# Casting x to bf16 in the load instead of on the engines, in a kernel of small attention blocks and a gated feed-forward stage

## The chip, the cores and the metric

The kernel runs on one core of a Trainium2 chip. Five engines work side by side, each through its own queue in order: PE (TensorE, matmuls and transposes), DVE (VectorE), ACT (ScalarE), POOL (GpSimd) and SP (SyncE, here only a queue for transfers). Data move between the chip's memory and the on-chip buffers by 16 DMA engines, which SP, ACT and POOL feed. A transfer that SP issues copies bytes as they are or transposes bf16 blocks; one that POOL issues can change the type on the way. The metric is the device time of one execution, in microseconds (us).

## The reference

There are two parts: an attention of x and a small state in both directions, batch by batch and head by head, and a gated feed-forward stage over all rows that come out. x is (8, 8, 512, 64): batch, head, token, width; state is (8, 8, 32, 64).

```python
scores = scale * x @ state^T          # (B, H, 512, 32)
xread  = softmax(scores) @ state      # (B, H, 512, 64)
scores2 = scale * state @ x^T         # the same products, transposed
sread  = softmax(scores2) @ x         # (B, H, 32, 64)
attn   = concat([xread, sread], axis=2)            # 544 rows for each head
x      = attn.transpose(0, 2, 1, 3).reshape(8 * 544, 512)
out    = (sigmoid(x @ w_gate) * (x @ w_val)) @ w_out   # 512 -> 1536 -> 512
```

Inputs and output are float32; the kernel computes its matmuls in bf16.

## The kernel before

**Tiling.** A batch is one unit of 512 token rows. Tokens lie as p*4 + c, with p the partition and c from 0 to 3. Heads go in pairs: j counts the four pairs, e the head in a pair. For each batch the kernel makes:

- xf, x in float32 (loaded by `load_x`), and xb, its bf16 copy with the heads in a row (`cast_x`; one call handles some of the heads on one engine);
- xT, its transpose: for batches 0 and 1 by PE (`xT_mm`) and a copy out of PSUM (`xT_cp`), from batch 2 on by SP's transposing transfers (`at_xT_dma`);
- the scores S (`S_mm`), with xT as the stationary operand and the moving one sTz, which is the state transposed with zeros so that a pair of heads gives two separate blocks; then exp on ACT (`S_exp`);
- Eb, the exponentials in bf16 (`at_Eb`, POOL), sums over the state's rows and their reciprocals (`n_sum`, DVE), the normalised a (`n_mul`) and its transpose aT (`aT_mm` and `aT_cp`, or by SP's transfers);
- SW, the state times the gate and value weights (`sw_mm`, called by `sw_visit` or `sw_wide`; copied out of PSUM by `sw_cp`), so that x's read never has to be formed: the gate and value inputs of a batch are aT times SW (`gv_mm`), followed by tanh (`gv_th`, ACT) and a product (`gv_glu`, DVE), and by the last matmul (`out_mm`);
- for the state's rows, sr (`sr_mm`, with Eb and xb), divided by the sums (`sr_fin`) into XS, which goes through the feed-forward stage at the end as "batch 8". For batch 1 the sums over tokens are first made on POOL (`p_tok`).

The state is loaded for two batches at a time (q counts these). For q = 0 it comes in float32 by ACT's queue and is cast; the others come as bf16 by POOL's queue (`load_sb`). `sT_mm` transposes it on PE by a matmul with the identity, and `sT_cp` or `sT_pad` copies it from PSUM into sTc (plain) or sTz (padded). `pad` copies sTc into sTz on POOL.

**The order.** The schedule is manual: the order in which the code calls these functions is the order in each engine's queue, and the framework adds the semaphores. Lines 434 to 652 write the order out by hand for batches 0 and 1 and the way into batch 2; the loop at line 654 runs the steady state, in which each batch's gv and out matmuls are interleaved with the next batch's preparation. PSUM tiles come from four pools, named GV (2 buffers), SWP (4), AT (1) and OU (1) in the calls, and a matmul into a buffer waits until its last reader is done. `warm` issues matmuls with no use of their own on PE before data are there. `gate` is a tiny POOL copy that reads one element, so that what POOL issues behind it waits for that element.

**Where the change and the steps of the prediction lie.** In the opening SP issues x of batches 0 and 1 in four parts each (lines 435 and 436), POOL casts a part of x and the state and then issues the weight loads, and DVE and ACT cast the other parts of x (lines 404 to 445). Lines 445 to 485 hold the first scores, Eb, the loads, the products `n_mul(1, ...)` on POOL and `aT_mm(1)`. Lines 503 to 555 hold the `sw_visit` calls, `sr_mm(1)`, `sT_mm(3)` and `sT_mm(1)`, and x of batch 2. Lines 576 to 599 lead to the first `out_mm` and the scores of batch 2.

Of the kernel before, what the change touches and what calls it, by code (L numbers as in the profile page):

```python
# [8 lines left out]
FP = mybir.dt.float32  # L9
BF = mybir.dt.bfloat16  # L10
# [6 lines left out]
def kernel(  # L17
# [14 lines left out]
    nc = tc.nc  # L32
# [32 lines left out]
    xfs, xbs, xTs = {}, {}, {}  # L65
# [4 lines left out]
    def load_x(b, eng, parts=1):  # L70
        xf = xfs[b] = stg.tile((128, H, 4, D), FP, name="xf")
        v, n = x[b].rearrange("h (p c) d -> p h c d", c=4), H // parts
        for i in range(parts):
            eng.dma_start(xf[:, n * i:n * i + n], v[:, n * i:n * i + n])  # L74

    def load_w(w, lo, n):
        src = (moe_w_gate, moe_w_val)[w].rearrange("(k p) n -> p k n", p=128)
        nc.gpsimd.dma_start((wg, wv)[w][:, :, lo:lo + n], src[:, :, lo:lo + n])

    def gate(landed):  # L80

        nc.gpsimd.tensor_copy(pre[:, 1:2], landed)
# [5 lines left out]
    def cast_x(b, cp, lo, n):  # L88
        if b not in xbs:
            xbs[b] = xp.tile((128, 4, H, D), BF, name="xb")  # L90
        cp(xbs[b].rearrange("p c h d -> p h c d")[:, lo:lo + n], xfs[b][:, lo:lo + n])  # L91


    def xT_tile(b):
# [6 lines left out]
    def xT_mm(b, j, place):  # L101

        ps = held["xT", b, j] = place[0].tile((128, 4, 128), BF, name="xTp", tag=place[1])
        for c in range(4):
            nc.tensor.transpose(ps[:, c], xbs[b][:, c, 2 * j:2 * j + 2].rearrange("p h d -> p (h d)"), ident)  # L105

    def xT_cp(b, j, cp):
        cp(xT_tile(b)[:, j], held["xT", b, j])  # L108
# [1 line left out]
    def at_xT_dma(b):  # L110
        xT = xT_tile(b)
        for c in range(4):
            nc.sync.dma_start_transpose(xT[:, :, c], xbs[b][:, c].rearrange("p h d -> p (h d)"))

    def S_mm(b, i, place, jjs=(0, 1)):
        if jjs[0] == 0:
            held["S", b, i] = place[0].tile((128, 4, 2, 2, Ns), FP, name="Sp", tag=place[1])
        ps = held["S", b, i]
        for jj in jjs:
            for c in range(4):  # L120
                nc.tensor.matmul(ps[:, c, :, jj], xTs[b][:, 2 * i + jj, c], sTz[:, b, 2 * i + jj], start=True, stop=True)  # L121

    def S_exp(b, i):
        if b not in E1s:
# [4 lines left out]
    def at_Eb(b):  # L129
        Ebs[b] = ap_.tile((128, 4, 2, 4, Ns), BF, name="Eb")  # L130
        for c in range(4):
            nc.gpsimd.tensor_copy(Ebs[b][:, c], E1s[b][:, c])  # L132
# [36 lines left out]
    def n_mul(b, i, eng, lo=0, n=4):  # L169
        if b not in abs_:  # L170
            abs_[b] = ap_.tile((128, 4, 2, 128), BF, name="ab")
        ri, ce = held["ri", b, i], slice(2 * lo, 2 * lo + 2 * n)
        eng.tensor_tensor(abs_[b].rearrange("p c e (j n) -> p (c e) j n", n=Ns)[:, ce, 2 * i:2 * i + 2],  # L173
                          halfE(b, i)[:, ce], ri[:, ce].unsqueeze(3).to_broadcast((128, 2 * n, 2, Ns)), ALU.mult)

    def aT_mm(b, place):
        ps = held["aT", b] = place[0].tile((128, 4, 2, 128), BF, name="aTp", tag=place[1])
        for c in range(4):
            for e in range(2):
                nc.tensor.transpose(ps[:, c, e], abs_[b][:, c, e], ident)  # L180
# [48 lines left out]

    sw_left = {}  # L230

    def sw_mm(pss, b, w, lo, n, o):
        for j in range(4):
            for e in range(2):
                rows = slice(e * 64, (e + 1) * 64)
                nc.tensor.matmul(pss[e][j * Ns:(j + 1) * Ns, o:o + n], sTc[rows, b, j] if b > 1 else sTz[rows, b, j, e],  # L236
                                 (wg, wv)[w][rows, j, lo:lo + n], start=True, stop=True)

    def sw_visit(b, lo, n, *ws):
# [126 lines left out]
    def cast_s(q, cp):  # L366
        sbs[q] = stg.tile((128, 1, 4, D), BF, name="sb", bufs=4)
        cp(sbs[q], sfs[q])

    def sT_mm(q, place):  # L370
        ps = stp[q] = place[0].tile((128, 4, 64), FP, name="stp", tag=place[1])
        for l in range(4):
            for e in range(2):
                nc.tensor.matmul(ps[e * 64:(e + 1) * 64, l], sbs[q][:, 0, l], ident_e[:, e], start=True, stop=True)
# [4 lines left out]
    def sT_pad(q, e, cp):  # L379

        rows = slice(e * 64, (e + 1) * 64)
        cp(sTz[rows, 2 * q:2 * q + 2, :, e].rearrange("p b j (u l) -> p (b j) u l", u=8),
           stp[q][rows].rearrange("p l (g u) -> p g u l", u=8))

    def pad(b, n=1):
        for e in range(2):
# [351 lines left out]
```

## Time and profile before

| | us |
|---|---|
| median of three runs | 226.21 (225.6 to 226.31) |
| the profiled execution | 226.03 |
| its span | 224.2 |
| PE busy in it | 217.0 (97%) |
| DVE busy | 140.7 (63%) |
| ACT busy | 127.6 (57%) |
| POOL busy | 48.8 (22%) |

The granted TensorE clock is 1.00 over the whole execution. The profile is one execution; its lines give times in us from the span's start. A line such as "11.23 1.44 POOL L132 CAST Eb<-E ... x4" is four instructions of line 132 on POOL that read E and write Eb, from 11.23 for 1.44 us; brackets behind it give the idle time in front of it and what ended that. A busy PE is modelled, so what counts on PE is where its stream stops. Landing times of transfers are counted from their issue.

### The profile page before, as it was taken

How to read it: one execution, taken by the hardware profiler on the slowest of the kernel's cores; microseconds unless marked ns; L12 is line 12 of the kernel's file. 1: busy time of each engine (PE TensorE's matmuls, PEld its weight loads, DVE VectorE, ACT ScalarE, POOL GpSimd, SP SyncE). 2: the span in 40 equal slices, each digit the busy share in tenths (PEclk: the TensorE clock that was granted, in tenths of full speed). 3: DMA queues.
4: the chain of work that ended last, by engine and by line, in shares of the span. 5: the costliest groups of instructions: out<-in, count | busy, mean ns of one | idle time of the engine just before them, and what ended most of it. 6: DMA issues, size and time to landing. Idle time of an engine off the chain costs nothing.

```text
span 224.2 us, 4791 instructions
## 1 busy us (share of the span) xinstructions
PE 217.0 (97%) x1859; PEld 111.2 (50%) x1859; DVE 140.7 (63%) x248; ACT 127.6 (57%) x239; POOL 48.8 (22%) x85
## 2 busy tenths in 40 slices
PE   7789999999999999999999999999999999999994
PEld 6654444444444545454444454454445444466744
DVE  3599897779368756885488648864787434422311
ACT  2587885645676557656675667556755444423311
POOL 3799560362041004200240006000200000000001
PEclk9999999999999999999999999999999999999999
DMA  6999989753898352627362521253122111111114
GB/s 188 289 201 206 280 130 179 114 193 78 147 292 274 71 151 76 219 59 126 100 225 50 121 96 61 44 81 117 47 78 66 50 50 47 67 73 48 50 26 114
DMA packets 38566, 27.37 MB, mean 122 GB/s; under 512 B 21168, under 2 KB 33840, under 8 KB 38544
## 3 DMA queue, kind: packets, MB, share of 16 engines
q1 hardware_dynamic: 31392, 19.74, 32.5%
q0 software_dynamic: 6864, 7.14, 17.6%
q8 instruction: 14, 0.23, 0.4%
q10 hardware_dynamic: 288, 0.20, 0.3%
q14 instruction: 8, 0.07, 0.1%
HBM read 18.35 MB, written 8.91 MB: 122 GB/s over the span
## 4 chain that ended last, share of the span: by engine, by line
PE 91%; DVE 3%; DMA 2%; ACT 1%; SPq 1%; issue 0%
PE outp L319 38%; PE gvp L288 37%; PE swp L236 5%; PE gvp L291 5%; DMA xf<-in_x_dram 2%; PE srp L213 1%; PE Sp L121 1%; PE outp L339 1%; DVE rs L139 1%; PE srp L210 1%; SPq L74 1%; DVE ab L173 1%; DVE ri L141 0%; DVE r L218 0%; PE xTp L105 0%; PE warm L353 0%
## 5 line engine op out<-in xcount | busy, mean ns | idle before, releaser
L303 DVE SCALAR_TENSOR_TENSOR glu<-th,gvp 128x512 bf16<-128x512 f32 (+1 forms) x108 | 69.9, 655 | 64.0 <-ACT th L298 48.7
L319 PE MATMUL outp<-wo,glu 128*128 128x512 bf16 x396 | 98.2, 379 | 0.0
L288 PE MATMUL gvp<-aT,SW 128*128 128x512 bf16 x384 | 96.3, 379 | 0.3 <-DVE aT L190 0.2
L298 ACT ACTIVATE th<-gvp 128x512 f32<-128x512 f32 (+1 forms) x108 | 61.8, 574 | 60.6 <-PE gvp L288 49.2
L288 PEld LDWEIGHTS <-SW 128*128 128x128 bf16 x384 | 36.3, 98 | 44.7 <-issue 3.1
L319 PEld LDWEIGHTS <-glu 128*128 128x128 bf16 x396 | 37.4, 98 | 40.8 <-issue 0.4
L274 ACT CAST SW<-swp 128x512 bf16<-128x512 f32 x70 | 38.8, 586 | 4.7 <-PE swp L236 3.3
L132 POOL CAST Eb<-E 128x256 bf16<-128x256 f32 x32 | 11.5, 407 | 89.9 <-ACT E L126 89.9
L323 ACT ACTIVATE res<-outp 128x512 f32<-128x512 f32 x33 | 19.7, 597 | 17.6 <-PE outp L319 17.6
L274 DVE CAST SW<-swp 128x512 bf16<-128x512 f32 x26 | 17.1, 683 | 1.6 <-PE swp L236 1.4
L91 POOL CAST xb<-xf 128x1024 bf16<-128x1024 f32 (+1 forms) x13 | 13.8, 1093 | 12.1 <-DMA xf<-in_x_dram 10.7
L330 POOL DMA_DIRECT2D out_dram<-res x2 | 1.1, 542 | 60.0 <-ACT res L323 60.0
L147 DVE TENSOR_REDUCE E<-E 128x128 f32<-128x512 f32 x12 | 12.4, 1035 | 0.0
L139 DVE TENSOR_REDUCE rs<-E 128x16 f32<-128x512 f32 x16 | 10.8, 676 | 1.3 <-ACT E L126 1.3
L126 ACT ACTIVATE E<-Sp 128x512 f32<-128x512 f32 x16 | 9.6, 604 | 2.4 <-PE Sp L121 2.4
L173 DVE TENSOR_TENSOR ab<-E,ri 128x512 bf16<-128x512 f32 x12 | 9.6, 804 | 0.0
L236 PE MATMUL swp<-wg,sTc 64*32 64x512 bf16 (+1 forms) x192 | 8.4, 328 | 0.0
L236 PEld LDWEIGHTS <-sTc 64*32 64x32 bf16 x384 | 4.5, 91 | 7.4 <-issue 4.7
L218 DVE RECIPROCAL r<-srp 128x128 f32<-128x128 f32 x8 | 7.6, 950 | 0.0
L121 PEld LDWEIGHTS <-xT 128*128 128x128 bf16 x128 | 5.5, 98 | 4.0 <-DVE xT L108 1.0
L236 PE MATMUL swp<-wv,sTc 64*32 64x512 bf16 (+1 forms) x192 | 7.4, 322 | 0.0
L291 PE MATMUL gvp<-XS,wg 128*128 128x256 bf16 x48 | 7.2, 273 | 0.0
(64 smaller groups left out, 122.0 us busy)
## 6 DMA issues: line engine op xcount, KB each, us to landing
out_dram<-res SPq DMA_DIRECT2D x31, 256.0 KB, 2.6
xf<-in_x_dram SPq DMA_DIRECT2D x12, 256.0 KB, 4.5
xf<-in_x_dram SPq DMA_DIRECT2D x3, 1024.0 KB, 6.8
wo<-in_moe_w_out_dram POOLq DMA_DIRECT2D x3, 512.0 KB, 5.9
wg<-in_moe_w_gate_dram POOLq DMA_DIRECT2D x2, 512.0 KB, 9.2
wv<-in_moe_w_val_dram POOLq DMA_DIRECT2D x2, 512.0 KB, 10.8
xf<-in_x_dram POOLq DMA_DIRECT2D x2, 512.0 KB, 10.4
xf<-in_x_dram POOLq DMA_DIRECT2D x1, 1024.0 KB, 9.2
```

The source lines that it names most:

```text
L91: cp(xbs[b].rearrange("p c h d -> p h c d")[:, lo:lo + n], xfs[b][:, lo:lo + n])
L139: nc.vector.tensor_reduce(rs, halfE(b, i), AX.X, ALU.add)
L147: nc.vector.tensor_reduce(held["E4", b][:, e].rearrange("p j n -> p (j n)"), E1s[b][:, :, e].rearrange("p c j n -> p (j n) c"), AX.X, ALU.add)
L173: eng.tensor_tensor(abs_[b].rearrange("p c e (j n) -> p (c e) j n", n=Ns)[:, ce, 2 * i:2 * i + 2], halfE(b, i)[:, ce], ri[:, ce].unsqueeze ...
L236: nc.tensor.matmul(pss[e][j * Ns:(j + 1) * Ns, o:o + n], sTc[rows, b, j] if b > 1 else sTz[rows, b, j, e], (wg, wv)[w][rows, j, lo:lo + n] ...
L274: cp(*sw_left.pop((b, lo, w, e)))
L288: nc.tensor.matmul(ps, SWs[b][:, g, w, fs], aTs[b][:, :, g], start=(g == 0), stop=(g == 1))
L291: nc.tensor.matmul(ps, (wg, wv)[w][:, j, fs], XS[:, j], start=(j == 0), stop=(j == 3))
L298: nc.scalar.activation(th, held["gv", b, f][0], AF.Tanh, scale=0.5)
L303: nc.vector.scalar_tensor_tensor(glus[b][:, f], held["th", b, f], 1.0, held["gv", b, f][1], ALU.add, ALU.mult)
L319: nc.tensor.matmul(ops[b, c], glus[b][:, f, c * 128:(c + 1) * 128], wo[:, f], start=(f == 0), stop=(f == NF - 1))
L323: nc.scalar.activation(res, ops[b, c], AF.Copy, scale=0.5)
```

## The change

The file has a second form of x in bf16, xc, laid out by head: (128, head, c, width). It is filled by `load_xc`, a POOL transfer that casts on the way. The table CP says which pairs of heads of which batch are held in that form: pairs 2 and 3 of batch 0, and all of batches 1 to 3. For these, SP issues no load, and xb is copied from xc on POOL at a later place, since `sr_mm` still reads it. The transposes read xc directly; with its layout a block of 128 columns holds two token positions of one head, not one token position of two heads, so `S_mm` takes another moving operand, sTd, with the head's state in both halves of the partitions, in separate column blocks. `sT_mm` makes both forms where both are needed, and `sT_dup` copies the new one out of PSUM. For q = 1 only the new form is made, and at another place in the order; sr_mm(1), wo's first load, some casts and the first three weight loads also stand in other places. The gate in front of the fourth weight load is gone.

```diff
+    CP = {0: (2, 3), 1: (0, 1, 2, 3), 2: (0, 1, 2, 3), 3: (0, 1, 2, 3)}
+    sTd = wp.tile((128, len(CP), H, 2, Ns), BF, name="sTd")
...
+    def load_xc(b, lo, n):
+        if b not in xcs:
+            xcs[b] = xp.tile((128, H, 4, D), BF, name="xc", bufs=len(CP))
+        v = x[b].rearrange("h (p c) d -> p h c d", c=4)
+        nc.gpsimd.dma_start(xcs[b][:, lo:lo + n], v[:, lo:lo + n])
...
     def cast_x(b, cp, lo, n):
-        cp(xbs[b].rearrange("p c h d -> p h c d")[:, lo:lo + n], xfs[b][:, lo:lo + n])
+        cp(xbs[b].rearrange("p c h d -> p h c d")[:, lo:lo + n],
+           (xcs[b] if lo // 2 in CP.get(b, ()) else xfs[b])[:, lo:lo + n])
...
     def xT_mm(b, j, place):
         for c in range(4):
-            nc.tensor.transpose(ps[:, c], xbs[b][:, c, 2 * j:2 * j + 2].rearrange("p h d -> p (h d)"), ident)
+            if j in CP.get(b, ()):
+                blk = xcs[b][:, 2 * j + c // 2, c % 2 * 2:c % 2 * 2 + 2].rearrange("p c d -> p (c d)")
+            else:
+                blk = xbs[b][:, c, 2 * j:2 * j + 2].rearrange("p h d -> p (h d)")
+            nc.tensor.transpose(ps[:, c], blk, ident)
...
     def at_xT_dma(b):
+            if b in CP:
+                nc.sync.dma_start_transpose(xT[:, c], xcs[b][:, 2 * c:2 * c + 2].rearrange("p h c d -> p (h c d)"))
...
     def S_mm(b, i, place, jjs=(0, 1)):
+                j, e, k = 2 * i + jj, c // 2, c % 2
+                if j in CP.get(b, ()):
+                    nc.tensor.matmul(ps[:, 2 * k:2 * k + 2, e, jj], xTs[b][:, j, c],
+                                     sTd[:, list(CP).index(b), 2 * j + e], start=True, stop=True)
...
     def sT_mm(q, place):
+        n = 0 if q == 1 else 32 if q == 0 else 64
+        if q < 2:
+            h0 = 64 - 8 * len(CP.get(0, ())) * 2 if q == 0 else 0
+            sd = stp[q, "d"] = ps[:, 4 * n:4 * n + 4 * (128 - h0)].rearrange("p (l g) -> p l g", l=4)
...
+                if n:
+                    nc.tensor.matmul(sz[rows, l], sbs[q][:, 0, l], ident_e[:, e, :n // 8], start=True, stop=True)
+                if q < 2:
+                    nc.tensor.matmul(sd[rows, l], sbs[q][:, 0, l], ident[:, h0:], start=True, stop=True)
...
+    def sT_dup(q, e, cp):
+        rows = slice(e * 64, (e + 1) * 64)
+        sd = stp[q, "d"][rows].rearrange("p l (g u) -> p g u l", u=8)
+        g = sd.shape[1]
+        hi = 8 * (2 * q + 2 - min(CP))
+        cp(sTd.rearrange("p b h e n -> p (b h) e n")[rows, hi - g:hi, e].rearrange("p g (u l) -> p g u l", u=8), sd)
...
     load_s(0, nc.scalar)
-    load_x(0, nc.sync, 4)
-    load_x(1, nc.sync, 4)
+    load_x(0, nc.sync, 4, 2)
     make_identity(nc, ident)
+    load_xc(0, 4, 4)
+    load_xc(1, 0, 4)
+    load_xc(1, 4, 4)
+    load_w(1, 256, 256)
+    load_w(0, 256, 256)
+    load_w(0, 0, 256)
...
+    nc.vector.memset(sTd, 0.0)
...
-    cast_x(0, pool, 0, 2)
+    cast_s(0, act)
+    cast_x(0, act, 0, 2)
...
-    cast_s(0, pool)
-    load_w(1, 256, 256)
     sT_mm(0, OU)
     sT_pad(0, 1, vec)
-    cast_x(0, act, 6, 2)
+    sT_dup(0, 0, vec)
+    sT_dup(0, 1, vec)
...
-    cast_x(0, act, 4, 2)
-    load_w(0, 256, 256)
-    load_w(0, 0, 256)
-    cast_x(1, vec, 2, 2)
-    gate(xfs[0][:, 7, 0, 0:1])
-    cast_x(1, act, 0, 2)
-    cast_x(1, vec, 4, 2)
-    cast_x(1, pool, 6, 2)
     at_Eb(0)
+    cast_x(0, pool, 4, 4)
...
     n_mul(1, 0, nc.gpsimd)
+    cast_x(1, pool, 0, 4)
+    cast_x(1, pool, 4, 4)
...
-    load_x(2, nc.gpsimd, 2)
+    load_xc(2, 0, 8)
+    load_wo(0)
     p_tok(1)
...
     sw_visit(0, 1024, 512, 0)
-    sr_mm(1, OU)
...
-    sT_mm(1, GV)
-    load_wo(0)
-    sT_cp(1, vec)
...
-    cast_x(2, act, 0, 4)
+    cast_x(2, pool, 0, 4)
     cast_x(2, pool, 4, 4)
     sw_visit(0, 512, 512, 1)
     gv_mm(1, 11, SWP)
+    sr_mm(1, OU)
...
     gv_glu(0, 7)
+    sT_mm(1, AT)
     gv_glu(0, 10)
+    sT_dup(1, 0, vec)
+    sT_dup(1, 1, act)
...
-    pad(2, 6)
+    pad(4, 4)
...
-    load_x(3, nc.gpsimd)
+    load_xc(3, 0, 8)
```

In the diff, lines of one function or stretch that lie apart are shown together. `sw_mm` takes the state of batches 1 to 3 from sTd as well.

More of the change, by code (lines that the diff above doesn't have):

```diff
@@ L120, in S_mm @@
             for c in range(4):
-                nc.tensor.matmul(ps[:, c, :, jj], xTs[b][:, 2 * i + jj, c], sTz[:, b, 2 * i + jj], start=True, stop=True)
+                j, e, k = 2 * i + jj, c // 2, c % 2
+                if j in CP.get(b, ()):
+                    nc.tensor.matmul(ps[:, 2 * k:2 * k + 2, e, jj], xTs[b][:, j, c],
+                                     sTd[:, list(CP).index(b), 2 * j + e], start=True, stop=True)
+                else:
+                    nc.tensor.matmul(ps[:, c, :, jj], xTs[b][:, j, c], sTz[:, b, j], start=True, stop=True)
     def S_exp(b, i):
@@ L230, with s_of @@
     sw_left = {}
+    def s_of(b, j, e):
+        rows = slice(e * 64, (e + 1) * 64)
+        if len(CP.get(b, ())) == 4:
+            return sTd[rows, list(CP).index(b), 2 * j + e, e]
+        return sTc[rows, b, j] if b > 1 else sTz[rows, b, j, e]
     def sw_mm(pss, b, w, lo, n, o):
@@ L235, in sw_mm @@
                 rows = slice(e * 64, (e + 1) * 64)
-                nc.tensor.matmul(pss[e][j * Ns:(j + 1) * Ns, o:o + n], sTc[rows, b, j] if b > 1 else sTz[rows, b, j, e],
+                nc.tensor.matmul(pss[e][j * Ns:(j + 1) * Ns, o:o + n], s_of(b, j, e),
                                  (wg, wv)[w][rows, j, lo:lo + n], start=True, stop=True)
@@ L370, in sT_mm @@
     def sT_mm(q, place):
-        ps = stp[q] = place[0].tile((128, 4, 64), FP, name="stp", tag=place[1])
+        n = 0 if q == 1 else 32 if q == 0 else 64
+        ps = place[0].tile((128, 512), FP, name="stp", tag=place[1])
+        sz = stp[q] = ps[:, :4 * n].rearrange("p (l g) -> p l g", l=4) if n else None
+        if q < 2:
+            h0 = 64 - 8 * len(CP.get(0, ())) * 2 if q == 0 else 0
+            sd = stp[q, "d"] = ps[:, 4 * n:4 * n + 4 * (128 - h0)].rearrange("p (l g) -> p l g", l=4)
         for l in range(4):
             for e in range(2):
-                nc.tensor.matmul(ps[e * 64:(e + 1) * 64, l], sbs[q][:, 0, l], ident_e[:, e], start=True, stop=True)
+                rows = slice(e * 64, (e + 1) * 64)
+                if n:
+                    nc.tensor.matmul(sz[rows, l], sbs[q][:, 0, l], ident_e[:, e, :n // 8], start=True, stop=True)
+                if q < 2:
+                    nc.tensor.matmul(sd[rows, l], sbs[q][:, 0, l], ident[:, h0:], start=True, stop=True)
     def sT_cp(q, cp):
@@ L381, in sT_pad @@
         rows = slice(e * 64, (e + 1) * 64)
-        cp(sTz[rows, 2 * q:2 * q + 2, :, e].rearrange("p b j (u l) -> p (b j) u l", u=8),
+        cp(sTz[rows, 0, :, e].rearrange("p j (u l) -> p j u l", u=8),
            stp[q][rows].rearrange("p l (g u) -> p g u l", u=8))
+    def sT_dup(q, e, cp):
+        rows = slice(e * 64, (e + 1) * 64)
+        sd = stp[q, "d"][rows].rearrange("p l (g u) -> p g u l", u=8)
+        g = sd.shape[1]
+        hi = 8 * (2 * q + 2 - min(CP))
+        cp(sTd.rearrange("p b h e n -> p (b h) e n")[rows, hi - g:hi, e].rearrange("p g (u l) -> p g u l", u=8), sd)
     def pad(b, n=1):
```

9 lines of the change are left out of this document (5 added, 4 removed).

## The prediction

> **What bounds the kernel now.** I read the page first for the engine that has no room, then the chain for where that engine begins to run without a pause, then the timelines around the two places that the change touches.
>
> ```profile
> PE 217.0 (97%) x1859; PEld 111.2 (50%) x1859; DVE 140.7 (63%) x248; ACT 127.6 (57%) x239; POOL 48.8 (22%) x85
> PE   7789999999999999999999999999999999999994
> DMA  6999989753898352627362521253122111111114
> ```
> PE is the bound, and only the first three slices (some 17 us) leave it idle. The profiled execution took 226.03 us, its span 224.2, so 1.83 us lie around the span. The median of the runs shown is 226.21, 0.18 higher. From 18 us on, the table by stretches shows PE busy all the time except 0.1 us near 28.3, up to the tail. So the time is: when PE's unbroken run starts, plus the work in that run, plus any new pause. The chain of waits (start, length, engine and line) shows what comes before the run:
>
> ```profile
> 2.27 5.24 DMA xf<-in_x_dram
> 7.53 0.63 ACT xb L91
> 8.21 0.40 PE xTp L105 x4
> 9.64 0.42 PE Sp L121 x8
> 10.09 0.60 ACT E L126
> 17.90 0.61 PE aTp L180 x8
> ```
> Batch 0's last x block lands at 7.5, is cast on ACT, transposed, scored at 9.64; after much DVE work PE starts aT_mm(1) at 17.90 and never stops. What holds aT_mm(1) is seen in the timelines of POOL and PE, which add the operation and, in brackets, the idle time before it and what ended it:
>
> ```profile
> 11.23 1.44 POOL L132 CAST Eb<-E 128x256 bf16<-128x256 f32 x4 [0.23 <-ACT E L126]
> 12.60 0.54 POOL L364 DMA_DIRECT2D sb<-in_state_dram  x1
> 13.13 0.75 POOL L78 DMA_DIRECT2D wg<-in_moe_w_gate_dram  x1
> 13.86 1.50 POOL L78 DMA_DIRECT2D wv<-in_moe_w_val_dram  x2
> 15.35 2.09 POOL L173 TENSOR_TENSOR ab<-E,ri 128x512 bf16<-128x512 f32 x2
> ...
> 15.92 0.30 PE L236 MATMUL swp<-wv,sTz 64*32 64x256 bf16 x8 [0.20 <-DMA wv<-in_moe_w_val_dram]
> 16.40 1.02 PE L288 MATMUL gvp<-aT,SW 128*128 128x512 bf16 x4 [0.18 <-DVE aT L190]
> ```
> POOL runs from E's end (11.2) to 17.44 with no hole; aT_mm(1) needs its last product. A weight load (15.92) and a DVE copy (16.40) stand only a little ahead of that. The third place is later:
>
> ```profile
> 25.27 0.41 PE L236 MATMUL swp<-wv,sTz 64*32 64x512 bf16 x8
> 25.50 0.40 PE L236 MATMUL swp<-wg,sTz 64*32 64x512 bf16 x8
> 25.83 0.40 PE L210 MATMUL srp<-Es,ones 128*128 128x128 bf16 x4
> 26.06 0.63 PE L213 MATMUL srp<-Eb,xb 128*128 128x64 bf16 x16
> 26.53 1.03 PE L288 MATMUL gvp<-aT,SW 128*128 128x512 bf16 x4
> 28.04 0.44 PE L374 MATMUL stp<-ident,sb 128*64 128x64 bf16 x16
> ...
> 25.75 1.07 ACT L274 CAST SW<-swp 128x512 bf16<-128x512 f32 x2
> 27.96 1.07 ACT L274 CAST SW<-swp 128x512 bf16<-128x512 f32 x2 [0.20 <-PE swp L236]
> ...
> 26.87 0.18 PEld L288 LDWEIGHTS <-SW 128*128 128x128 bf16 x2 [0.25 <-ACT SW L274]
> ```
> The matmul of sw_visit(1, 512, 512, 1) at 25.27 lets ACT cast from 25.75 to 26.83, and gv_mm(1, 7)'s third matmul must wait for that cast: its weights load at 26.87, just in time. PE's 0.70 us of sr_mm(1) at 25.83 fills exactly this wait. Likewise the 0.13 us of sT_mm(1) at 28.2 (half of the sixteen) ends as ACT's cast at 27.96 frees the buffers of the next gv_mm, at 28.55.
>
> **The change, part by part.**
>
> *First x block.* SP issues two parts instead of eight. POOL is free at 1.30 (identity done) and issues heads 4 to 7. Lower bound of the landing: load_wo(1), on a nearly idle queue, took 5.9 us from issue for twice the bytes; the extra 256 KB at the 200 GB/s seen from 10 to 16 us are 1.3, so 4.6, hence 5.9. Upper: the first weight load of the same size, with x beside it, took 6.4, hence 7.7. Here only 640 KB of SP's and ACT's loads stand beside it, and the middle, 6.9, is taken. The ACT casts (0.62 each) leave that path: transposes and their end 0.8 after landing, 7.7.
>
> *DVE in front of the scores.* Before, two pads of 64x256 took 0.86. Now two pads of half that and two copies of 64x384 from PSUM: 128x256 took 0.41 and 128x512 0.69, so about 0.28 and 0.55 each, 1.66. From the end of DVE's cast (5.46) that is 7.1; two copies of xT (0.74) 7.85; the third (0.42) 8.27. So DVE, not the load, decides: scores at 8.3 against 9.64, 1.35 earlier (at a landing of 7.7, 0.7). The state's cast and one x cast on ACT, idle until 7.53, and the second memset (0.91) on DVE, idle from 2.2 to 4.9, cost nothing. Sixteen instead of eight state matmuls lie in the time when PE runs warm-ups.
>
> *POOL.* Ahead of E it now has eight loads of 0.75, done by 7.5, without the gate. After E (now 9.9) come Eb 1.37, the new cast_x(0) of 128x1024 (1.04 for f32 to bf16 in this trace; a bf16 copy of 64x768 took 0.84, so no cheaper), the state 0.53, three loads 2.22, two products 2.09: 17.15 instead of 17.44. So 1.04 of the 1.35 are spent here, 0.3 is left. Behind the products wait batch 1's two casts (2.03), the state loads, x of batch 2, and p_tok(1) with Eb(1), done about 27; their reader sr_mm(1) comes after 31, and sr_fin(1) frees its buffer from 38.7 on as before. wo's first part goes ahead of p_tok(1); its reader starts at 40.26.
>
> *Weights.* POOL's queue, whose first packets came 3.3 after the issue at 5.12 (at 8.5 by the transfers in short windows), now moves from about 4.6, with x in front: 1.83 MB up to the fourth weight load at 0.2 MB/us is 13.8, and that load's lag behind its bytes before was 1.5: 15.3 against 15.9. PE could then begin aT_mm(1) near 17.2, so POOL (17.15 plus the 0.45 seen from its end to the first matmul) still ends last: 17.6 against 17.90. **Start: -0.3**, bounds +0.35 (late landing) and -0.7 (weights).
>
> *sr_mm(1) moved* behind gv_mm(1, 11), where PE's 44 matmuls from 30.75 to 40.05 follow without a gap. There it costs its whole length, 0.70 (between 53.71 and 54.40 its like takes 0.69). Where it leaves, PE waits for ACT instead. Bounds 0 (if ACT came ahead) and 0.70; ACT's cast hangs on PE's own matmul at 25.27, so **+0.70**.
>
> *sT_mm(1) moved* and widened to 128 columns. Its old place gains nothing (ACT's end at 28.55 holds the next matmul). In the new one: 0.31 from a 512-column matmul into such a group (20.75 to 21.05), three steps of 0.056, 0.31 out (28.29 to 28.60), less the 0.22 of one step: 0.57; at least 0.22. Taken: **+0.57**. Its two copies (0.7 on DVE, 0.6 on ACT) stand where DVE idles 1.0 us near 35.3 and replace sT_cp(1) and ACT's cast of x, 1.04.
>
> *Rest.* Batch 2's and 3's transposes by DMA no longer wait for a cast; scores of batch 2 stand at 41.98 and had their xT at 39.5. POOL's pads, x of batch 3 in bf16 and the other weight rows keep their shapes and lie beside PE: 0.
>
> Sum: -0.30 + 0.70 + 0.57 = +0.97, so 226.03 + 0.97 = 227.0.
>
> **Two rules.** The Trainium skill, "DMA: Bandwidth & Descriptors", Anatomy of one DMA, gives a load issued from GpSimd about 2.0 us plus bytes over 436 GB/s; an estimate by it for load_wo(1), 1 MB read, is 4.4, and the trace has 5.9, so the rule is short by 1.5 here. By it the landing would be 4.5, rival B would fall away, and the sum would stay 227.0, since DVE decides. "SBUF — State Buffer", Who interferes with whom, says that a DVE copy in a two-port mode shuts GpSimd out; DVE's x cast beside POOL's took 0.54 against 0.42 here, which agrees. By it that cast, now beside POOL's descriptor writing, would shift the weights by up to 0.5 and give 227.2.
>
> **Rivals.**
> A, the forecast: 226.6 to 227.6.
> B, heads 4 to 7 land late. For it: the 6.4 us row. Against: less stands beside it. From 7.0 on each us counts; at 7.7 the scores gain 0.7, POOL's cast costs 1.04, the start loses 0.35: 226.03 + 0.35 + 1.27 = 227.65.
> C, not slower: ACT's cast at 25.75 comes ahead, so that sr_mm(1) covered nothing. It decides if that cast ends 0.5 us or more earlier against PE. Against it: ACT was idle 0.1 before it, waiting for PE. Time 226.03 - 0.3 + 0.57 = 226.3.
> D, POOL's cast isn't last, since its spans are rough: start -0.7, 226.03 - 0.7 + 1.27 = 226.6.
> E, the whole 1.35 of the scores reaches aT_mm(1) (POOL not last, and the weights' lag 0.8 instead of 1.5, as the first x part's was) and C holds, with sT_mm(1) at 0.22: 226.03 - 1.35 + 0.22 = 224.9; faster.
>
> **Numbers.** A 0.58, B 0.18, C 0.08, D 0.06, E 0.10. A measurement of this kernel tells about 0.3% (0.7 us) from no change: 225.5 to 226.9. Of A two thirds lie above 226.9. Slower: 0.39 + 0.18 = 0.57; same: 0.19 + 0.08 + 0.06 = 0.33; faster 0.10. The range runs from between C and E to beyond B: 225.9 to 228.2; A's own is 226.6 to 227.6.
>
> **What would show it.** Scores of batch 0 near 8.3, with DVE's xT copies just ahead; POOL busy from 9.9 to 17.2 and aT_mm(1) released by it near 17.6; an idle PE of about 0.7 before the third matmul of gv_mm(1, 7), released by ACT; srp matmuls after 31 with no idle time ahead. The prediction is wrong if PE's run starts before 17 or after 18.3, if that 0.7 isn't there, or if PE pauses anew between 31 and 45, where xT of batch 2, the state copies or wo come late.

## The result, and the profile after

The changed kernel takes 228.65 us (median of 4 runs, 228.41 to 229.9), the kernel before 225.91 (4 runs, 225.23 to 226.31): ratio 1.0136, 95% interval 1.0089 to 1.0183. The change costs 2.7 us. Two of its four executions, 228.85 and 229.9, ran at a mean granted clock of 0.99, the other two, 228.41 and 228.45, at 1.00. The sign was forecast; the size was not, since 228.65 lies above the range. The profiled execution took 228.41 us with a span of 226.6: 2.38 us more than the profiled execution of before.

The page of the changed kernel, busy time and two rows by slices:

```profile
PE 217.8 (96%) x1867; PEld 111.2 (49%) x1867; DVE 143.1 (63%) x249; ACT 126.9 (56%) x238; POOL 52.4 (23%) x87
PE   7779899899999999999999999999999999999994
DMA  6999989593799253527471421244122111111113
```

PE's work rose by only 0.8 us; the rest is idle time: slices 3, 5 and 8 are each a tenth less busy than before, all others as they were. The chain of waits (start, length, engine and line) names the places:

```profile
10.42 1.44 POOL Eb L154 x4
11.86 0.99 POOL xb L100
...
14.79 12.78 DMA wv<-in_moe_w_val_dram
...
32.13 0.47 PE srp L235 x16
...
38.44 0.60 DVE sTd L428
39.04 0.02 issue
39.06 0.59 ACT sTd L428
...
44.45 1.02 PE outp L347 x4
```

PE's own timeline, with the idle time before each group in brackets, gives the pauses:

```profile
25.41 0.40 PE L264 MATMUL swp<-wg,sTz 64*32 64x512 bf16 x8
25.74 0.60 PE L316 MATMUL gvp<-aT,SW 128*128 128x512 bf16 x2
26.79 0.61 PE L316 MATMUL gvp<-aT,SW 128*128 128x512 bf16 x2 [0.45 <-ACT SW L302]
27.61 0.41 PE L264 MATMUL swp<-wv,sTz 64*32 64x512 bf16 x8 [0.21 <-DMA wv<-in_moe_w_val_dram]
...
31.97 0.63 PE L235 MATMUL srp<-Eb,xb 128*128 128x64 bf16 x16
32.44 5.34 PE L316 MATMUL gvp<-aT,SW 128*128 128x512 bf16 x24
37.71 0.41 PE L411 MATMUL stp<-ident,sb 128*64 128x128 bf16 x8
...
44.45 1.02 PE L347 MATMUL outp<-wo,glu 128*128 128x512 bf16 x4 [0.57 <-DVE glu L331]
```

Setting the start of each matmul against the same matmul of before gives the account of the two profiled executions:

| Place (time before) | shift so far | added here |
|---|---|---|
| gv_mm(0, 3) (16.41), aT_mm(1) (17.90) | -0.09 | -0.09 |
| sw_visit(0, 1024, 512, 1) (27.49), waits for the last wv load | +0.12 | +0.21 |
| after sr_mm(1) (31.75 after) | +0.81 | +0.69 |
| after sT_mm(1) (37.71 after) | +1.25 | +0.44 |
| out_mm(0, 7) (42.45), waits for DVE's glu | +2.00 | +0.75 |
| PE's last matmul (221.13) | +2.00 | 0 |
| end of the span | +2.4 | +0.4 |

Everything happens before 45 us or in the last 4. From out_mm(0, 7) on, the two kernels run in step.

### The profile page after: what moved, and what is told of

It reads as the page before. It is cut to its first block, busy times and chain, and to the rows that moved or that the text cites. A ratio compares the mean times of both kernels' runs of the same rounds, so it can differ in the third digit from the quotient of the medians.

```text
span 226.6 us, 4794 instructions
## 1 busy us (share of the span) xinstructions
PE 217.8 (96%) x1867; PEld 111.2 (49%) x1867; DVE 143.1 (63%) x249; ACT 126.9 (56%) x238; POOL 52.4 (23%) x87
## 4 chain that ended last, share of the span: by engine, by line
PE 83%; DMA 7%; DVE 4%; POOL 2%; ACT 2%; issue 0%; SPq 0%; DVEq 0%
PE outp L347 37%; PE gvp L316 32%; DMA wv<-in_moe_w_val_dram 6%; PE gvp L319 5%; PE swp L264 4%; DVE glu L331 2%; DMA xf<-in_x_dram 2%; PE srp L235 1%; PE outp L367 1%; PE Sp L143 1%; DVE sTd L428 1%; PE srp L232 1%; POOL Eb L154 1%; ACT th L326 1%; ACT E L148 0%; POOL xb L100 0%
## 5 line engine op out<-in xcount | busy, mean ns | idle before, releaser
L100 POOL CAST xb<-xf 128x1024 bf16<-128x1024 f32 x8 | 9.5, 1229 | 2.0 <-DMA xf<-in_x_dram 2.0
L100 POOL COPY xb<-xc 128x1024 bf16<-128x1024 bf16 x7 | 7.1, 1048 | 5.7 <-PE swp L264 3.9
L319 PE MATMUL gvp<-XS,wv 128*128 128x256 bf16 x48 | 7.2, 273 | 0.0
L381 PE MATMUL warm<-ones 128*128 128x128 bf16 x63 | 5.6, 262 | 1.0 <-DVE ones L448 1.0
L319 PEld LDWEIGHTS <-wg 128*128 128x128 bf16 x48 | 4.7, 98 | 2.5
```

The source lines that it names most:

```text
L100: cp(xbs[b].rearrange("p c h d -> p h c d")[:, lo:lo + n], (xcs[b] if lo // 2 in CP.get(b, ()) else xfs[b])[:, lo:lo + n])
L319: nc.tensor.matmul(ps, (wg, wv)[w][:, j, fs], XS[:, j], start=(j == 0), stop=(j == 3))
```

## The experiments

### Two displaced steps of PE

**sr_mm(1) late, in the kernel before.**

```diff
     sw_visit(0, 1024, 512, 0)
-    sr_mm(1, OU)
...
     gv_mm(1, 11, SWP)
+    sr_mm(1, OU)
```

> The kernel before, with one call moved: sr_mm(1) stands behind gv_mm(1, 11), as in the changed kernel. Theory (its old place was free, because PE waits there for ACT's cast; the new one is not): PE idles 0.6 to 0.7 us before the third matmul of gv_mm(1, 7) near 26.9, the srp matmuls stand near 30.9 with no wait ahead, every later PE matmul starts 0.69 us later, and the time is 226.6 to 226.8 where the kernel before has 225.9 to 226.1. Rival (moving it costs nothing, the loss in the changed kernel comes from late transfers): PE's later matmuls stand where they were, time unchanged.

225.96 us (6 runs) against 225.16 (9 runs): ratio 1.0041 (1.0016 to 1.0066). PE's timeline:

```profile
25.90 0.60 PE L288 MATMUL gvp<-aT,SW 128*128 128x512 bf16 x2 [0.45 <-ACT SW L274]
...
30.80 0.63 PE L213 MATMUL srp<-Eb,xb 128*128 128x64 bf16 x16
```

The wait for ACT's cast appears where sr_mm(1) left, and sr_mm(1) costs its full length at its new place: the shift against the first profile goes from -1.05 to -0.35, +0.70. The predicted term (+0.70) holds, by itself and in the changed kernel (+0.69).

**sT_mm(1) back beside sT_mm(3), both copies on ACT after sT_cp(3).**

```diff
     sT_mm(3, AT)
+    sT_mm(1, OU)
...
     sT_cp(3, act)
+    sT_dup(1, 0, act)
+    sT_dup(1, 1, act)
...
-    sT_mm(1, AT)
...
-    sT_dup(1, 0, vec)
-    sT_dup(1, 1, act)
```

> The changed kernel, with sT_mm(1) back beside sT_mm(3) near 28.2, in the OU buffer, and its two copies on ACT behind sT_cp(3). Theory (the new place of sT_mm(1) cost 0.44 us on PE and 0.75 by the wait of ACT's copy; the old one is hidden by ACT's cast): PE's matmuls from 45 on stand 1.1 to 1.2 us earlier than in the changed kernel, the time is 227.2 to 227.4. Rival (the copies cost as much wherever they stand, since ACT and DVE are full near 30): PE pauses anew between 30 and 34 and the time stays within 0.4 of the changed kernel's.

227.17 us (4 runs; before 225.16), ratio 1.0099 (1.0073 to 1.0124). Against the changed kernel PE stands 0.21 earlier at 28.7, 0.65 earlier at 38.1 and 1.40 earlier from 45.3 on: 0.44 for the matmuls and 0.75 for the late out_mm(0, 7) are gone, and 0.21 is the wait for the last wv load, absent here. What is left over the profiled before is +0.61 at PE's last matmul: sr_mm(1), less 0.09 by which PE stands earlier ahead of it (28.50 against 28.59). So 0.44 and 0.75 both hang on this one step. (The medians lie 2.0 apart, the two profiled spans 1.0: the profiled before was one of the longer executions, see below.)

**Why out_mm(0, 7) is late.** In the kernel before, the last of the three products ahead of out_mm(0, 7) ends at 42.22, 0.23 before the matmul that needs it:

```profile
40.34 1.88 DVE L303 SCALAR_TENSOR_TENSOR glu<-th,gvp 128x512 bf16<-128x512 f32 x3
...
42.45 1.03 PE L319 MATMUL outp<-wo,glu 128*128 128x512 bf16 x4
```

ACT and DVE in the changed kernel around the two copies (operation sTd<-stp):

```profile
38.35 0.68 DVE L428 CAST sTd<-stp 64x512 bf16<-64x512 f32 x1
38.96 0.67 DVE L331 SCALAR_TENSOR_TENSOR glu<-th,gvp 128x512 bf16<-128x512 f32 x1
39.06 0.58 ACT L428 CAST sTd<-stp 64x512 bf16<-64x512 f32 x1 [1.08 <-DVE sTd L428]
39.67 0.60 ACT L326 ACTIVATE th<-gvp 128x512 f32<-128x512 f32 x1
40.30 0.69 DVE L331 SCALAR_TENSOR_TENSOR glu<-th,gvp 128x512 bf16<-128x512 f32 x1 [0.68 <-ACT th L326]
```

The two copies write disjoint halves of sTd, yet ACT's starts only when DVE's is done: ACT idles 1.08, th(1, 4) stands behind that copy in ACT's queue, DVE's next glu waits 0.68 for this th, and the glu that out_mm(0, 7) reads comes late. The two copies also read one PSUM buffer, and this is the likelier reason for the wait: at 7.96 to 8.55 ACT copies into batch 0's xT, and DVE begins to copy into another part of the same tile at 8.35, each out of its own PSUM buffer. No run tests it. Two runs split the 0.75. Both copies on ACT:

```diff
-    sT_dup(1, 0, vec)
+    sT_dup(1, 0, act)
     sT_dup(1, 1, act)
```

> The changed kernel, with sT_dup(1, 0) on ACT instead of DVE, so that ACT's copy no longer waits for DVE's. Theory (PE's idle time of 0.57 us before out_mm(0, 7) at 44.46 comes from tanh(1, 4) standing behind ACT's copy, which waits for DVE's copy, which stands behind two products): tanh(1, 4) starts near 39.2 instead of 39.68, DVE has one copy less, and out_mm(0, 7) starts about 0.45 us earlier; later PE matmuls 0.45 earlier, time 227.9 to 228.1 beside 228.4 to 228.6. Rival (DVE is simply too full there): DVE drops 0.6 us and all of the 0.57 goes. Second rival (out_mm(0, 7) waits for something else, such as the scores' exp): no change.

228.06 us (4 runs; before 225.16), ratio 1.0148 (1.0096 to 1.0199). PE was 0.57 earlier before this place and 0.89 after it: 0.32 of the 0.75 came back, since ACT now has 1.17 of copies ahead of th(1, 4). ACT's copy first:

```diff
-    sT_dup(1, 0, vec)
     sT_dup(1, 1, act)
+    sT_dup(1, 0, vec)
```

> The changed kernel with the two copies of sT_mm(1) in the other order: ACT's is issued first, DVE's second; engines, sizes and places stay. Theory (the late out_mm(0,7), +0.75, comes from ACT's copy waiting for DVE's, 39.06 instead of right behind th(1,5), and not from the copies' length): ACT copies at about 37.9 in that trace's time, th(1,4) stands at 38.5 to 38.8 instead of 39.67, DVE's copy waits for nothing, and from out_mm(0,7) on PE stands 0.5 to 0.75 earlier; time 0.4 to 0.8 below the changed kernel's, ratio to before 1.008 to 1.013. Rival (the two copies are simply work too much for ACT and DVE there): less than 0.2 gained. With both copies on ACT 0.32 was gained.

228.19 us (4 runs; before 225.53, 7 runs), ratio 1.0099 (1.0066 to 1.0133). ACT and DVE:

```profile
39.16 0.58 ACT L428 CAST sTd<-stp 64x512 bf16<-64x512 f32 x1 [0.18 <-PE stp L411]
39.76 0.60 ACT L326 ACTIVATE th<-gvp 128x512 f32<-128x512 f32 x1
39.77 0.68 DVE L428 CAST sTd<-stp 64x512 bf16<-64x512 f32 x1 [0.34 <-ACT sTd L428]
40.38 1.27 DVE L331 SCALAR_TENSOR_TENSOR glu<-th,gvp 128x512 bf16<-128x512 f32 x2
```

Now DVE waits, 0.34, for ACT. This execution started late; at out_mm(0, 7) its shift against the changed kernel falls from +0.99 to +0.65, so 0.34 came back, less than the 0.5 to 0.75 I expected and more than the rival's 0.2. So the order of the two copies is worth about half of the 0.75. The other half I put down to the work itself: DVE is left no idle time there but the 0.34, and has 0.68 more to do. No run separates that half alone; in the old place, with both copies on ACT, the whole 0.75 is gone.

### The start

**Half of batch 1's x not loaded** (heads 0 to 3 stand in for heads 4 to 7).

```diff
-                blk = xcs[b][:, 2 * j + c // 2, c % 2 * 2:c % 2 * 2 + 2].rearrange("p c d -> p (c d)")
+                blk = xcs[b][:, (2 * j + c // 2) % (4 if b == 1 else 8), c % 2 * 2:c % 2 * 2 + 2].rearrange("p c d -> p (c d)")
...
-    load_xc(1, 4, 4)
...
-    cast_x(1, pool, 4, 4)
+    pool(xbs[1].rearrange("p c h d -> p h c d")[:, 4:8], xcs[1][:, 0:4])
```

> The changed kernel, with half of batch 1's x not loaded: heads 4 to 7 of batch 1 are computed from heads 0 to 3, so that 512 KB less are read ahead of the weights. Theory (the weight loads land no earlier than before since x takes their place in the same queue; POOL with its new cast is a second limit close behind): the fourth weight load lands 1.0 to 1.3 us earlier, PE's wait for it at 15.98 goes, aT_mm(1) still stands at 17.7 to 17.9 since POOL's second product ends at 17.6, and the wait for the last weight load at 27.6 goes: time 0.2 to 0.3 below the changed kernel. Rival (only the weights hold the start): aT_mm(1) at 16.8 to 17.1 and the time about 1 us below.

228.09 us (4 runs; before 225.16), ratio 1.0129 (1.0114 to 1.0145). The fourth weight load no longer holds PE (its sw matmul at 15.15 instead of 15.98), but aT_mm(1) stands at 17.91, 0.1 later than in the changed kernel, waiting 0.29 for POOL's product. The wait at 27.6 is gone, which gives most of the 0.37 that PE's last matmul gains (it is absent too in four runs that keep this load, see the step "Rest: 0" below). So earlier weights alone don't move the start.

**No cast by POOL at all**: sr_mm reads the copy by head, in two matmuls of 64 columns where one of 128 was.

```diff
-    cast_x(0, pool, 4, 4)
-    cast_x(1, pool, 0, 4)
-    cast_x(1, pool, 4, 4)
...
+                    for e in range(2):
+                        rows = slice(e * 64, (e + 1) * 64)
+                        nc.tensor.matmul(sr[rows, j, e], xcs[b][:, 2 * j + e, c], Eb[:, c, e, j],
+                                         start=(c == 0), stop=(c == 3))
```

> The changed kernel with no cast of x by POOL at all: sr_mm reads the bf16 copy by head directly, with twice as many matmuls of 64 columns each. Theory 1 (POOL's cast of batch 0's heads 4 to 7, 1.04 us between Eb and the weight loads, is what ate the start's gain): the products end about 1.0 earlier than the 17.64 of the changed kernel, and aT_mm(1) then stands at 17.1 to 17.3, held by the fourth weight load (landed 15.97, PE waited 0.34 for it) instead of 17.8; time 0.5 to 0.7 below the changed kernel's, less what sr_mm loses by its narrower stationaries (three groups of 32 instead of 16 matmuls, at most 0.3 each). Theory 2 (POOL isn't last, the weights' landing alone sets the start): aT_mm(1) stays within 0.2 of 17.8 and the time is no lower than the changed kernel's. In both, the pauses at gv_mm(1,7), the displaced sr_mm(1), sT_mm(1) and the late out_mm(0,7) stay.

229.12 us (4 runs; before 225.82, 7 runs), ratio 1.0166 (1.0131 to 1.0201). PE's timeline:

```profile
13.10 0.30 PE L270 MATMUL swp<-wg,sTz 64*32 64x256 bf16 x8 [0.31 <-DMA wg<-in_moe_w_gate_dram]
...
16.34 1.02 PE L322 MATMUL gvp<-aT,SW 128*128 128x512 bf16 x4 [0.26 <-DVE aT L212]
...
17.83 0.61 PE L202 MATMUL aTp<-ident,ab 128*128 128x128 bf16 x8
```

POOL's products end at 16.7, 0.9 earlier, and aT_mm(1) is where it was, 17.83. (PE's last matmul is 0.48 later: the narrow matmuls cost 0.24 more for each of batches 1 to 3, and some 0.25 come back, since the wait at 27.6 is absent here.) My first theory, that POOL's cast ate the gain, falls. A second chain ends at the same place: the first weight load (PE waits for it at 13.10), then in PE's order sw, sr_mm(0) and aT_mm(0), then ACT's and DVE's copies of aT, then gv_mm(0, 3) at 16.34. Behind its copy of aT DVE has a reciprocal and two products, the last of which aT_mm(1) waits for (see the step "Start" below).

**Both at once**: no cast, and half of batch 1's x left out.

> The changed kernel without POOL's casts of x (sr_mm reads the copy by head) and with heads 4 to 7 of batch 1 not loaded: heads 0 to 3 stand in for them, so that 512 KB less are read ahead of the weights; this leaves out half of batch 1's x. Alone, neither moved aT_mm(1) by more than 0.1. Theory 1 (three limits end within 0.3 us of each other: POOL's products, the weight loads that hold the first matmuls of sw in PE's order, and the copies of aT that follow those): with POOL and the weights relieved together the first sw matmul stands at 12.4 to 12.8, gv_mm(0,3) at 15.4 to 15.8 and aT_mm(1) at 16.8 to 17.2, 0.6 to 1.0 earlier. Theory 2 (something else, further back, sets aT_mm(1)): it stays at 17.6 to 17.9.

One run, 228.05 us. PE's timeline:

```profile
12.23 0.30 PE L270 MATMUL swp<-wg,sTz 64*32 64x256 bf16 x8
...
15.47 1.02 PE L322 MATMUL gvp<-aT,SW 128*128 128x512 bf16 x4 [0.57 <-DVE aT L212]
...
16.96 0.61 PE L202 MATMUL aTp<-ident,ab 128*128 128x128 bf16 x8
```

aT_mm(1) stands 0.85 earlier, as the first theory has it; alone, the two had moved it by +0.02 and +0.10. But 0.36 of the 0.85 are there before either limit: this execution has its scores at 8.47, the changed kernel at 8.83. Counted from the scores, aT_mm(1) gains 0.48, and 0.04 and 0.11 in the two runs before. So POOL's queue and the weight loads end close together here, and in this one execution only relieving both moves the start.

**The first part of the change alone**: the kernel before, with only batch 0's heads 4 to 7 by POOL's queue. The rest of the changed opening comes with it: the weight loads go out from 2.38 on (in the kernel before from 5.12), the gate is gone, and ACT casts the state.

```diff
-    load_x(0, nc.sync, 4)
+    load_x(0, nc.sync, 4, 2)
     load_x(1, nc.sync, 4)
...
+    load_xc(0, 4, 4)
+    load_w(1, 256, 256)
+    load_w(0, 256, 256)
+    load_w(0, 0, 256)
...
+    sT_dup(0, 0, vec)
+    sT_dup(0, 1, vec)
...
     at_Eb(0)
+    cast_x(0, pool, 4, 4)
```

> The kernel before with one part of the change alone: heads 4 to 7 of batch 0's x are loaded and cast by POOL's queue, scored from the state copy on both halves, and cast into the layout by token on POOL after Eb; batches 1 to 3, sr_mm(1) and sT_mm(1) as before. My prediction gave the start -0.30 against the one profiled execution of the kernel before. Theory 1 (the profiled execution of before had its x land late; an undisturbed one has scores at 8.67, and the front costs DVE two copies of 0.55 and POOL a cast of 1.04): scores at 8.8 to 9.2, aT_mm(1) 0.5 to 1.2 later than in an undisturbed execution of before, time +0.4 to +1.2 us, ratio 1.002 to 1.005. Theory 2 (the start really gains 0.1 to 0.3 as predicted): ratio 0.998 to 1.000.

228.86 us (4 runs; before 225.82), ratio 1.0152 (1.0117 to 1.0186): worse than either theory. PE's timeline:

```profile
9.81 0.40 PE L119 MATMUL xTp<-ident,xc 128*128 128x128 bf16 x4 [2.67 <-DMA xc<-in_x_dram]
...
11.19 0.63 PE L140 MATMUL Sp<-sTd,xT 128*128 128x64 bf16 x8
```

The same load, issued at 1.46, lands at 9.8 instead of 7.4. What differs beside it is SP's queue, which here moves 1.4 MB in the first 10 us (six loads of x) and in the changed kernel 0.5 MB (two). aT_mm(1) stands at 20.48, 2.58 later than in the profiled before: 1.60 are there at the transposes (9.81 against 8.21), and POOL's cast of 1.04 stands ahead of its products, for the last of which aT_mm(1) waits 0.29. So in this run POOL's cast does cost its length.

The page of this run has a row that no profile above it has:

```profile
PEclk9979999999999999999999999999999999999999
```

Behind PE's pause of 2.67 the granted clock is 0.50 from 10.6 to 14.1 us; all four executions of this run have a mean of 0.99. On the way to aT_mm(1) it costs little here: from the transposes to the end of batch 0's exponentials it takes 3.14 us, and 2.97 in the kernel before.

**The converse**: all of batch 0's x by SP, batches 1 to 3 by POOL's queue, without casts, with sr_mm(1) and sT_mm(1) as in the next run.

```diff
-    CP = {0: (2, 3), 1: (0, 1, 2, 3), 2: (0, 1, 2, 3), 3: (0, 1, 2, 3)}
+    CP = {1: (0, 1, 2, 3), 2: (0, 1, 2, 3), 3: (0, 1, 2, 3)}
-    load_x(0, nc.sync, 4, 2)
+    load_x(0, nc.sync, 4)
-    load_xc(0, 4, 4)
```

> As the run before it, and all of batch 0's x is loaded by SP in f32 and cast on ACT and DVE as before the change; only batches 1 to 3 go by POOL's queue. SP then carries 1 MB, not 2.1 MB, beside batch 0. Theory 1 (the last piece of batch 0's x lands by how much is on its way ahead of it): SP's fourth piece lands at 6.3 to 6.6 and the scores begin at 8.4 to 8.7, which is level with the best execution seen of the kernel before (8.67) and 0.1 to 0.4 ahead of the changed kernel; POOL has no cast behind Eb; aT_mm(1) at 16.5 to 16.9; time 0.5 below to 0.3 above the kernel before, the 0.37 at the end among it. Theory 2 (the weights now stand behind 512 KB of x in POOL's queue and land later than before): fourth weight load after 16.3, aT_mm(1) after 17.2, time 0.5 or more above the kernel before.

230.02 us (4 runs; before 225.82), ratio 1.0185 (1.0145 to 1.0226). ACT:

```profile
9.42 1.14 ACT L100 CAST xb<-xf 128x512 bf16<-128x512 f32 x2 [4.71 <-DMA xf<-in_x_dram]
```

The time is on the side of the second theory, but the reason isn't the one it named: SP's last pieces of batch 0 land at 9.4, though SP has half as much to move as before. In the kernel before, POOL's first weight load is issued at 5.1 and x lands at 6.6 to 7.8; here POOL issues its loads from 1.47 on. The landing isn't all of it: behind PE's pause of 3.34 the granted clock is 0.50 from 10.9 to 14.3, the sixteen transposes of batch 1 take 1.88 (0.83 and 0.38 in the kernel before), and the shift against the profiled before grows from 1.88 at 10.09 to 2.59 at the first sw matmul. Three of the four executions have a mean clock of 0.993 and take 230.0 to 230.27; the fourth has 1.00 and takes 228.54. In these two runs whatever shares the first 8 us with batch 0's x delays it, on either queue. That agrees with the Trainium skill, "DMA: Bandwidth & Descriptors", Queues, rings and completion order, by which each DMA engine takes turns between the queues that have work; how the turns were shared isn't visible in these runs.

**The kernel before, once more.**

> The kernel before, unchanged, profiled once more, to see how much its start moves from one execution to another. Theory 1 (the landing of the last pieces of batch 0's x varies, and the execution that I took as the base had it late): scores at 8.6 to 9.0 instead of 9.64, aT_mm(1) at 17.0 to 17.3 instead of 17.90, span 223.2 to 223.7 instead of 224.2. Theory 2 (the start of the first profile is the rule, and the run with sr_mm(1) late was the exception): scores at 9.5 or later, span 224.0 or more.

One run, 226.25 us, span 224.5: scores at 9.88, so the first theory fell for this execution. ACT's first cast of the late pieces, here and in the run with sr_mm(1) late, whose start is the same code:

```profile
7.77 1.14 ACT L91 CAST xb<-xf 128x512 bf16<-128x512 f32 x2 [5.06 <-DMA xf<-in_x_dram]
```

```profile
6.56 1.14 ACT L91 CAST xb<-xf 128x512 bf16<-128x512 f32 x2 [3.86 <-DMA xf<-in_x_dram]
```

The landing moves by 1.2 us from execution to execution, and PE's start with it (gv_mm(0, 3) at 15.84, 16.41 and 16.64 in three profiles). Of the 23 timed spans of before in the three comparisons, 15 lie at 223.1 to 223.7 and 8 at 224.0 to 224.5: my base, 224.2, was one of the longer third. In five executions with the changed start gv_mm(0, 3) stands at 16.10, 16.32, 16.39, 16.70 and, with the first weight load late, 17.59.

### The displaced steps undone, and the end

**No casts, sr_mm(1) at its old place, sT_mm(1) ahead of sw_visit(0, 512, 512, 1) with both copies on ACT.**

```diff
     sw_visit(0, 1024, 512, 0)
+    sr_mm(1, OU)
...
     gv_glu(1, 1)
+    sT_mm(1, AT)
+    sT_dup(1, 0, act)
+    sT_dup(1, 1, act)
```

> The same, with sr_mm(1) back in its place of before (behind sw_visit(0,1024,512,0)) and sT_mm(1) ahead of sw_visit(0,512,512,1), its two copies on ACT. Theory: against the kernel before sr_mm(1) gives back 0.69, sT_mm(1) with its copies 1.2; what is left over the kernel before is the start (0 to +0.4) and the 0.37 at the end: 0 to +0.8 us, ratio 1.000 to 1.004. Rival (the loss comes from something that lasts all through the kernel, such as wider matmuls or slower transfers, and only shows at those places): the ratio stays above 1.008.

227.81 us (4 runs; before 225.82), ratio 1.0105 (1.0074 to 1.0136), outside my 1.000 to 1.004. PE's timeline:

```profile
26.36 0.68 PE L238 MATMUL srp<-Eb,xc 128*64 128x32 bf16 x32
...
30.87 0.41 PE L417 MATMUL stp<-ident,sb 128*64 128x128 bf16 x8
```

Against the profiled before: start +0.21, sr_mm(1) with 32 narrow matmuls instead of 16 +0.24, sT_mm(1) +0.36 (it still stands between other PE work), sr_mm(2) and sr_mm(3) +0.25 each, the end some +0.4. The ratio is on the rival's side of 1.008, but the time is lost in named places and PE runs in step between them, so a loss all through is not what the trace shows; I had left out what the narrow matmuls and sT_mm(1) cost. The displaced sr_mm(1) and the late out_mm(0, 7) are gone, as expected.

**Six more loads on SP.** After PE's last matmul starts, the span goes on for 3.07 us before and 3.47 after. In the trace's semaphore events SP closes with a row of waits, 0.06 apart where nothing is awaited; in the kernel before the last landing is the last wait (223.34), in the changed kernel six more stand behind it (225.38 to 225.75).

```diff
     load_xc(3, 0, 8)
+    junk = wp.tile((128, 6, 64), FP, name="junk")
+    for i in range(6):
+        nc.sync.dma_start(junk[:, i], x[3][i, 0:128])
```

> The changed kernel with six small loads (32 KB each, read by nobody) added to SP's queue in the middle, beside the load of batch 3's x, so that SP issues as many transfers as in the kernel before. Theory (the 0.37 us at the end come from the order in which SP's closing waits go round the semaphores: in the changed kernel six waits of 0.06 stand behind the one for the last landing, in the kernel before none): from the start of PE's last matmul to the end of the span it takes 3.0 to 3.15 us, as in the kernel before (3.07), instead of 3.47. Rival (the last stores themselves land later): 3.4 or more. The rest of the trace stays as in the changed kernel.

One run, 228.1 us: 3.09 us instead of 3.47, and the last landing is again the last wait. So the 0.4 at the end come from the order of the closing waits (six of 0.06 make 0.37), which the number of SP's transfers shifts: the change leaves SP six fewer.

No version here beats the kernel before.

## Why the prediction was wrong

**What held.** PE stays the bound, and the loss is in new pauses and displaced PE work before 45 us. sr_mm(1): +0.70 predicted, +0.69 in the changed kernel and +0.70 alone. Rival C (ACT's cast early, so that sr_mm(1) covered nothing) is out: the pause of 0.45 stands at 26.79, ended by ACT (by the starts it is 0.62: the third matmul stands 1.05 behind the first, where 0.43 is usual; 0.7 was forecast). sT_mm(1): +0.57 predicted, +0.44 measured; its old place gained nothing, as said (PE waits 0.24 for ACT at 28.71).

**Step "Its two copies ... stand where DVE idles 1.0 us near 35.3 and replace sT_cp(1) and ACT's cast of x": cost 0, measured +0.75.** This is the largest miss. The idle time named was not where the copies stand (38.4 to 39.6), and the prediction has no wait between the two. ACT's waited for DVE's, with th(1, 4) behind it in the queue: turning the order and putting both on ACT gave back 0.34 and 0.32, moving the copies away all of it. In the kernel before, out_mm(0, 7) had 0.23 to spare, and I didn't ask who reads what is queued behind the copies. The prediction did name the sign, a new pause of PE between 31 and 45 where the state copies come late, but gave it no price.

**Step "Start: -0.3": measured -0.09 against the same base.** The scores came at 8.83, not 8.3: the load landed at 7.37 instead of 6.9, and its transposes began at 7.54, when DVE's copies of the state gave their buffer free. The fourth weight load held PE until 15.98, not 15.3. And "POOL ... still ends last" was wrong: POOL's timeline,

```profile
10.42 1.44 POOL L154 CAST Eb<-E 128x256 bf16<-128x256 f32 x4 [2.82 <-ACT E L148]
11.80 1.04 POOL L100 COPY xb<-xc 128x1024 bf16<-128x1024 bf16 x1
...
15.54 2.09 POOL L195 TENSOR_TENSOR ab<-E,ri 128x512 bf16<-128x512 f32 x2
```

ends at 17.64, where 17.15 was predicted, and aT_mm(1) doesn't wait for it. The 0.45 that the prediction added behind POOL's end was time to spare: where aT_mm(1) does wait for POOL (half of batch 1's x, both copies on ACT), it starts 0.06 behind POOL's end, at 17.91 and 17.69. What ends its wait, by the trace's semaphore events, is DVE's queue, whose last two products read the PSUM buffer that aT_mm(1) writes next:

```profile
15.84 0.42 DVE L212 COPY aT<-aTp 128x512 bf16<-128x512 bf16 x1
16.18 0.95 DVE L240 RECIPROCAL r<-srp 128x128 f32<-128x128 f32 x1
17.16 0.59 DVE L248 TENSOR_TENSOR XS<-srp,r 64x128 bf16<-64x128 f32 x2
17.80 0.61 PE L202 MATMUL aTp<-ident,ab 128*128 128x128 bf16 x8
```

The products end at 17.75, and at 17.84 in the kernel before, where aT_mm(1) starts at 17.90. Ten of the fourteen profiles have it so; in three POOL's product comes last, in one PE itself was still busy. So already in the kernel before DVE's queue set the start, not POOL. Without POOL's casts that queue ended at the same time (17.78), since DVE's copy of aT stood idle 0.51 for ACT's, which the first weight load had made late. The prediction had read the 15.92 and 16.40 rows as "only a little ahead" and then let that chain move earlier with the weights; it didn't.

**Base.** The sum stood against one execution whose x landed late. Measured against the early one (sr_mm(1) late), the changed start is behind: the sw matmul that stands at 21.80 in the base stands at 20.82 there, and at 21.4 to 22.1 in four of the five executions with the changed start. How much the start costs on average isn't settled with three profiles. sr_mm(1), sT_mm(1), its copies and the end sum to some 2.3 of the 2.74 between the medians; the 0.4 or so that is left holds the start, the late load of the next paragraph and the two executions at a clock of 0.99, and no run parts these.

**Step "Rest: 0".** The term that was missing is the end, +0.4, which nothing in the profile of before announced. In the profiled execution the last wv load, too, issued at 14.79 instead of 14.60 (POOL was busy with its cast), took 12.8 us and came 0.21 too late; in the base it had about a microsecond in hand (landed 26.3, read at 27.49). But four other profiles have the same loads in the same order (both copies on ACT, sT_mm(1) back, ACT's copy first, six loads on SP); there it took 11.8 to 12.6 us, and PE didn't wait for it. So these 0.21 are rather the luck of one execution.

**The two rules.** By the Trainium skill, "DMA: Bandwidth & Descriptors", Anatomy of one DMA, heads 4 to 7 would have landed at 4.5, an estimate; they landed at 7.37, and at 9.8 beside SP's six loads, so the rule for one load by itself is short here, further than in the row of before. By the Trainium skill, "SBUF — State Buffer", Who interferes with whom, DVE and GpSimd exclude each other in some operations. DVE's cast took 0.73 here beside POOL's two issues of 1.52, and 0.43 in the run without POOL's casts, where those issues took 1.62: one of the two waits, which agrees. DVE's two products took 1.43 in the changed kernel and 1.76 in the run with both copies on ACT, beside POOL's cast, and 1.28 in the kernel before, which agrees too. So POOL's cast lengthens DVE's queue, the one that holds aT_mm(1). The 0.5 that the weights were to lose by it doesn't show.

## What to carry to other kernels

A copy moved to two engines isn't free because each has idle time: look at whether the two copies wait for each other, at what is queued behind each, and who reads that. When several chains end within 0.3 us of each other, taking away one gives nothing; ask of each what would end next, and of matmuls in order, which load the first of them waits for. A load that becomes early on one queue is paid by what shares the DMA engines with it in the same microseconds, and a base taken from one execution carries the luck of its landings. The end of one transfer or product and the start of the matmul behind it don't show a wait by being close: look for a run in which the one does hold the other, and take the distance there.

## What the runs showed that I had not expected

- 256 KB written as bf16 by POOL's queue at the start took 5.9 us with 0.5 MB on SP's queue and 8.3 us with 1.4 MB; SP's last piece of batch 0 that the scores wait for landed at 6.6 to 7.8 where POOL's loads began at 5.0 to 5.2, and at 9.4 where they began at 1.5.
- SP's closing waits take 0.06 us each, one behind the other, so six transfers fewer made the end 0.4 us longer, and six small ones put back made it short again.
- In two profiles PE stood idle for 2.67 and 3.34 us in the opening, and the granted clock fell to 0.50 for some 3.4 us soon after. In the twelve others, where the longest pause of PE ahead of 45 us is 1.41, it stayed at 1.00 there. That the pause is the cause is inferred.
- Splitting a matmul group's 128 columns into two of 64 raised sr_mm by 0.24 to 0.25 us per batch at the same arithmetic.
- The landing of batch 0's x, with the same code in the opening, moved by 1.2 us between three executions, and aT_mm(1) with it by 0.8 to 1.0.
